# Local attention scores as 64-column products of two heads, sums by column halves, and a new order of steps

## The chip, the core and the metric

The kernel runs on one core of a Trainium2 chip. Five engines work side by side, each with its own queue of instructions: TensorE (PE; its loads of stationary weights are shown apart as PEld), VectorE (DVE), ScalarE (ACT), GpSimd (POOL) and SyncE (SP), which here issues nearly all DMA transfers. The metric is the device time of one execution in microseconds.

## The reference

Eight batches of eight heads, 576 positions, 64 features per head. Attention has two parts that are added, and then a mixture of experts works on the 4,608 tokens of 512 features:

```python
    out_d = sm_attn(q_d, k_d, v_d)          # q, k, v averaged over groups of 4: 144 positions
    out_up = np.repeat(out_d, factor, axis=2)
    mask = np.abs(pos[:, None] - pos[None, :]) < factor
    scores = scale * np.matmul(q, k.transpose(0, 1, 3, 2))
    scores = np.where(mask, scores, -1000000000.0)
    ...
    out_local = np.matmul(attn, v)          # each position sees 7 neighbours
    return (out_up + out_local)
    ...
    logits = x @ w_gate                     # 8 experts, each takes 576 tokens in order of the logits
    h = np.maximum(x[mask] @ w1[e], 0.0); out[mask] = h @ w2[e]
```

## The kernel before

The program has two stages. The first is the whole attention with the router's logits; it is what the change touches. The second routes the tokens and runs the eight experts, and begins on TensorE at 271.8 us of the profiled span.

**What the attention does per batch.** q and k arrive with positions on partitions and are turned by TensorE (`trw`, L291; the last 64 positions by `trt`, L318). ACT or DVE bring them out of PSUM (`evac`, L268 and L270; the last positions L326 and L333): k goes into `kt`, with the even head of a pair on partitions 0 to 63 and the odd one on 64 to 127; q goes into `qz`, which has a plane for each of the two heads and zeros in the other head's partitions, so that a product over 128 partitions gives one head's scores. `gsum` (L257, L260) adds groups of four positions of q and k: DVE for batch 0, POOL for the rest of q. The averaged attention, here called the means, is `down_s` (products L346, L349), `down_t` (transposes L382, L386) and `down_v` (products with the averaged v, L405, L408, L416), then a store to DRAM.

**What it does per unit.** The local part is cut into 36 units u of four windows of 32 queries by 38 keys, for all eight heads. `loc_s`: a bf16 product (L485) writes the mask for all 128 rows and 304 columns into PSUM, then 32 fp32 products (L492) add the scores, each for one head and one window: 32 columns of weights, 38 moving columns, at one of four column strips of the array. DVE takes the maximum (L502) and subtracts it (L508), ACT exponentiates (L511). `loc_t` transposes the result (L521), ACT brings it out (L529). `loc_v` multiplies with v (L544, 64 weight columns by 65), DVE normalizes (L555, L557). `log_a` adds the means, `logits` transposes the sum (L583), ACT copies it (L589), and products with 64 weight columns and 8 moving ones (L597) give the logits.

**How products count in the trace.** An fp32 product stands in the trace as two MATMUL records, each with its own weight load; a transpose or a bf16 product is one. So the 36 x 32 score products are 2,304 records. In the trace a form such as `128*32` gives the rows and columns of the array that an instruction uses; by it there are three kinds here: 128, 64 and 32 columns wide. Where two neighbours in TensorE's queue differ in that width, this text speaks of a border.

**What sets the order.** Every piece of work is a stream of steps, with a rank for each step in the table `KEYS`: `S_u`, `T_u`, `V_u` are `loc_s`, `loc_t`, `loc_v` of unit u; `X_u` the logits; `B`, `C`, `E` with a part and a batch are `down_s`, `down_t`, `down_v`; `R` and `Q` the transposes of q and k; `N` and `W` the loads. The planner always runs the step with the least rank, after whatever it needs, and each engine's queue holds the instructions in that order: in the attention this fixes the order on PE, DVE, ACT, POOL and SP alike. Engines take their queues strictly in order, so a step that is ranked too early holds up all behind it.

## Time and profile before

| | us |
|---|---|
| three runs | 731.86, 738.87, 736.12; median 736.12 |
| profiled execution | 733.37, of which 731.7 are the span that the trace shows |
| attention on TensorE | 0 to 271.8 |
| TensorE busy over the span | 662.4 (91%) |

The trace gives for each engine what it did and when; times in it count from the start of the span. Busy time of TensorE is the union of its records, which overlap, so the price of a product is better read from the distance between the starts of consecutive groups than from the duration of one record. "Idle before" names what ended the idle time of an engine; "issue" is idle time in which the engine waited for nothing that the profile shows.

### The profile page before, as it was taken

What the parts mean: (1) busy time and instruction counts of PE and PEld (TensorE: products, weight loads), DVE (VectorE), ACT (ScalarE), POOL (GpSimd) and SP (SyncE); (2) the same over time, 40 slices, a digit from 0 to 9 for tenths busy, and PEclk for the clock granted to TensorE, in tenths of its full rate; (3) what the DMA queues carried; (4) which work ended last, traced back from release to release, by engine and by line L of the source; (5) the groups of instructions that cost most, each with busy time, mean ns of one, the idle gap of its engine ahead of it and who ended that gap; (6) DMA issues with size and microseconds to landing.
All of it is one profiled execution on the core that took longest, in us unless ns stands there. A gap on an engine that the chain in (4) does not pass through costs nothing.

```text
span 731.7 us, 21463 instructions
## 1 busy us (share of the span) xinstructions
PE 662.4 (91%) x8833; PEld 473.0 (65%) x8833; DVE 492.2 (67%) x1363; ACT 346.6 (47%) x673; POOL 244.6 (33%) x296
## 2 busy tenths in 40 slices
PE   6898989899988983499999999999999999999994
PEld 4777779798867872376476576575576565674651
DVE  4876756587575756879889889698797895410300
ACT  6587757578776540433533525344253265411210
POOL 7578072835637350400612312230230441101011
PEclk9799998999999995589999999999999999999998
DMA  7899889997996560715726565182651998101001
GB/s 214 214 221 256 257 239 240 260 281 207 272 226 174 166 191 11 249 47 191 210 58 220 152 232 144 67 301 67 220 169 52 336 260 204 37 1 44 22 29 37
DMA packets 142813, 123.98 MB, mean 169 GB/s; under 512 B 86836, under 2 KB 117044, under 8 KB 142716
## 3 DMA queue, kind: packets, MB, share of 16 engines
q1 hardware_dynamic: 135256, 100.82, 48.0%
q0 software_dynamic: 6512, 21.24, 9.0%
q8 instruction: 70, 1.15, 0.7%
q10 hardware_dynamic: 948, 0.55, 0.3%
q14 instruction: 27, 0.22, 0.1%
HBM read 93.09 MB, written 21.23 MB: 156 GB/s over the span
## 4 chain that ended last, share of the span: by engine, by line
PE 52%; issue 16%; DVE 15%; POOL 5%; DMA 5%; ACT 4%; SPq 1%; POOLq 0%; DVEq 0%; ACTq 0%
PE pX L1296 13%; PE pH L1241 12%; PE o L544 4%; PE g L492 3%; PE g L291 3%; PE pR L786 2%; DVE ht L1273 2%; PE g L583 2%; POOL out_dram L1317 2%; PE g L521 2%; PE g L597 2%; PE g L346 2%; DVE cmp L753 2%; DMA nat<-in_k_dram 2%; PE g L408 2%
## 5 line engine op out<-in xcount | busy, mean ns | idle before, releaser
L1241 PE MATMUL pH<-xt,wh 128*128 128x256 f16 (+1 forms) x1024 | 194.0, 288 | 3.8 <-DVE ht L1273 2.9
L1296 PE MATMUL pX<-wh,ht 128*128 128x512 f16 (+1 forms) x640 | 183.1, 379 | 0.9 <-ACT y L1313 0.9
L1241 PE MATMUL pH<-xt,wl 128*128 128x256 f16 (+1 forms) x512 | 147.5, 288 | 0.0
L1296 PEld LDWEIGHTS <-ht 128*128 128x128 f16 (+1 forms) x960 | 80.4, 100 | 88.1 <-issue 3.7
L1296 PE MATMUL pX<-wl,ht 128*128 128x512 f16 (+1 forms) x320 | 119.0, 380 | 0.0
L1317 POOL DMA_INDIRECT out_dram<-y,idx x40 | 40.8, 1021 | 226.2 <-ACT y L1313 195.9
L1241 PEld LDWEIGHTS <-wh 128*128 128x128 f16 x1024 | 95.2, 98 | 31.2 <-DVE ht L1273 5.2
L1269 ACT ACTIVATE ht<-pH 128x512 f16<-128x512 f32 (+1 forms) x128 | 45.5, 407 | 116.1 <-PE pH L1241 103.8
L1273 DVE SCALAR_TENSOR_TENSOR ht<-pH,ht 128x512 f16<-128x512 f32 (+1 forms) x128 | 52.3, 449 | 64.4 <-ACT ht L1269 64.2
L1158 DVE SCALAR_TENSOR_TENSOR wl<-nat,wh 128x512 f16<-128x512 f32 x128 | 86.1, 684 | 1.2 <-ACT wh L1155 0.5
L1313 ACT ACTIVATE y<-pX 128x512 f32<-128x512 f32 (+1 forms) x40 | 23.7, 595 | 99.3 <-PE pX L1296 40.9
L1155 ACT ACTIVATE wh<-nat 128x1024 f16<-128x1024 f32 x64 | 67.0, 1054 | 6.2 <-DMA nat<-in_moe_w_dram 5.3
L1182 POOL DMA_INDIRECT xg<-x_dram,idx x40 | 45.6, 1140 | 62.0 <-DVE idx L1062 29.0
L1241 PEld LDWEIGHTS <-wl 128*128 128x128 f16 x512 | 50.4, 98 | 13.5 <-issue 0.4
L529 ACT COPY pt<-g 64x512 f32<-64x512 f32 x72 | 41.8, 580 | 20.4 <-PE g L521 19.4
L291 PE MATMUL g<-ident,nat 128*128 128x128 f32 x256 | 40.3, 294 | 7.5 <-DMA nat<-in_k_dram 4.9
L544 PE MATMUL o<-vw,pt 128*64 128x65 f32 x1152 | 44.3, 227 | 2.8 <-DVE gtmp L257 2.0
L544 PEld LDWEIGHTS o<-vw,pt 128*64 128x64 f32 x1152 | 38.7, 139 | 6.3 <-issue 4.0
L492 PEld LDWEIGHTS g<-kt,qz 128*32 128x32 f32 x2304 | 26.7, 113 | 20.9 <-issue 18.1
L492 PE MATMUL g<-kt,qz 128*32 128x38 f32 x2304 | 32.8, 205 | 7.9 <-issue 5.9
L291 PEld LDWEIGHTS g<-ident,nat 128*128 128x128 f32 x256 | 30.4, 149 | 11.2 <-issue 3.6
L225 POOL TENSOR_TENSOR gtv<-nat 128x512 f32<-128x512 f32 x16 | 21.4, 1338 | 46.6 <-DMA nat<-in_v_dram 24.3
(215 smaller groups left out, 1119.8 us busy)
## 6 DMA issues: line engine op xcount, KB each, us to landing
nat<-in_moe_w_dram SPq DMA_DIRECT2D x28, 1024.0 KB
vw<-in_v_dram SPq DMA_DIRECT2D x136, 78.0 KB
up<-up_dram SPq DMA_DIRECT2D x36, 256.0 KB
x_dram<-x SPq DMA_DIRECT2D x36, 256.0 KB
nat<-in_q_dram SPq DMA_DIRECT2D x16, 512.0 KB
nat<-in_k_dram SPq DMA_DIRECT2D x16, 512.0 KB
nat<-in_v_dram SPq DMA_DIRECT2D x16, 512.0 KB
up_dram<-xu SPq DMA_DIRECT2D x16, 128.0 KB
```

The lines of the kernel that those rows point to most:

```text
L291: nc.tensor.transpose(p[:, a, :, fp], src[:, 4 * hh + 2 * a + s, 2 * fp:2 * fp + 2].rearrange("p f d -> p (f d)"), self.ident)
L492: nc.tensor.matmul(sv[32 * a:32 * a + 32, 4 * g + c], self.qz[b % 2][:, h // 2, h % 2, QW * w:QW * w + QW], self.kt[b][:, h // 2, key0(w): ...
L529: nc.scalar.copy(out[r, :, :, a], p[r].rearrange("p (i h q) -> p i h q", h=4, q=QW))
L544: nc.tensor.matmul(o[64 * i:64 * i + 64, g, 65 * h:65 * h + 65], pt[:, 2 * g + i, h].rearrange("p b q -> p (b q)"), self.vw[u % 4][:, i, 4 ...
L1155: nc.scalar.activation(hi, r, AF.Copy, scale=sc)
L1158: nc.vector.scalar_tensor_tensor(lo[:, a:a + LOP], r[:, a:a + LOP], sc, hi[:, a:a + LOP], op0=OP.mult, op1=OP.subtract)
L1182: self.fetched = self.nc.gpsimd.indirect_dma_start(out=xg[:n], out_offset=None, in_=self.x, in_offset=bass.IndirectOffsetOnAxis(ap=idx[:n, ...
L1241: nc.tensor.matmul(p[:, s, :s1 - s0], self.w[k, d][a][:, 128 * f:128 * f + 128], self.xt[k][:, b, d, s0:s1], start=j == 0, stop=j == len(s ...
L1269: nc.scalar.activation(hi, q, AF.Relu)
L1273: nc.vector.scalar_tensor_tensor(lo, q, 0.0, hi, op0=OP.max, op1=OP.subtract)
L1296: nc.tensor.matmul(p[o:o + m], self.ht[k][:, f, h0:h0 + m], self.w[k, 4 + f // 2][b][:, 512 * (f % 2):512 * (f % 2) + 512], start=j < part ...
L1317: i = nc.gpsimd.indirect_dma_start(out=self.out, in_=y[:n], in_offset=None, out_offset=bass.IndirectOffsetOnAxis(ap=plan.vals["idx", k][:n ...
```

## The change

`qz` is laid out anew: per head pair and window, the 32 queries of the even head and then the 32 of the odd head lie side by side. A score product takes both as 64 columns of weights, against the same 38 keys; the zeros keep the heads apart, and the rows of the result stand where they stood. A unit has 16 score products instead of 32. The mask product of a unit, and the two kinds of products in `down_v` that were 128 columns wide (L405 and L408), are each issued as two products of 64 columns, for rows 0 to 63 and 64 to 127. The writers and readers of `qz` follow its layout: `evac` of q writes runs of 16 elements (each second one of a window of 32) instead of one run of 256; the copies of the last positions become two of 8 groups each instead of one of 16; the first addition of `gsum` reads window by window. And 505 rows of `KEYS` are written anew: all of the attention's but a dozen. The ranks of routing and experts are as before.

In the changed kernel line numbers after L250 are up to 10 higher: L291 becomes L292, L318 L324, L346 L353, L382 L389, L405 L414, L408 L418, L416 L426, L485 L496, L492 L502, L521 L531, L544 L554, L583 L593, L597 L607.

```diff
--- before.py
+++ after.py
@@ -82,7 +82,8 @@
         self.sd = cst.tile([128, 9, G], F32, name="sd")
         self.sdt = cst.tile([128, 2 * H, GT], F32, name="sdt")
         for i in range(2):
-            for name, n, l in (("qz", S, self.qz), ("qdz", 128, self.qdz), ("qdt", G - 128, self.qdt)):
+            self.qz.append(cst.tile([128, HP, NW, 2, QW], F32, name=f"qz{i}"))
+            for name, n, l in (("qdz", 128, self.qdz), ("qdt", G - 128, self.qdt)):
                 l.append(cst.tile([128, HP, 2, n], F32, name=f"{name}{i}"))
 
 
@@ -99,8 +100,8 @@
         nc = self.nc
 
         def heads(a, b, t):
-            a.memset(t[:64, :, 1], 0.0)
-            b.memset(t[64:, :, 0], 0.0)
+            for e, r, s in ((a, slice(0, 64), 1), (b, slice(64, 128), 0)):
+                e.memset(t[r, :, :, s] if len(t.shape) == 5 else t[r, :, s], 0.0)
 
         if part == 0:
             for t in self.vw[:2]:
@@ -249,12 +250,12 @@
                 self.kdt[b] = self.wk.tile([128, HP, G], F32, name="kdt")
             parts = [(slice(0, 128), self.kt[b], [(self.kdt[b], 0, G)])]
         else:
-            parts = [(slice(64 * s, 64 * s + 64), self.qz[b % 2][:, :, s],
+            parts = [(slice(64 * s, 64 * s + 64), self.qz[b % 2][:, :, :, s],
                       [(self.qdz[b % 2][:, :, s], 0, GM), (self.qdt[b % 2][:, :, s], GM, G)]) for s in range(2)]
         for i, (r, src, dst) in enumerate(parts):
             tmp = self.wk.tile([128, GW, 2 * G], F32, name="gtmp", bufs=1)[r]
             sv = src[r, a:a + GW]
-            eng.tensor_tensor(tmp, sv[..., ::2], sv[..., 1::2], op=OP.add)
+            eng.tensor_tensor(tmp.rearrange("p a (w i) -> p a w i", w=NW) if which == "q" else tmp, sv[..., ::2], sv[..., 1::2], op=OP.add)
             for d, g0, g1 in dst:
                 t = tmp[..., 2 * g0:2 * g1]
                 eng.tensor_tensor(d[r, a:a + GW], t[..., ::2], t[..., 1::2], op=OP.add)
@@ -298,10 +299,15 @@
         if which == "q":
             self.need(("fixed", b % 2))
         r = slice(64 * s, 64 * s + 64)
-        t = self.qz[b % 2][r, 2 * hh:2 * hh + 2, s] if which == "q" else self.dest(b)[r, 2 * hh:2 * hh + 2]
         for par in range(2):
-            self.evac(8 * b + 4 * hh + 2 * s + "qk".index(which) + 1, t[:, :, par:4 * GM:2],
-                      p[64 * par:64 * par + 64].rearrange("p a i f -> p a (i f)"))
+            src = p[64 * par:64 * par + 64]
+            if which == "q":
+                out = self.qz[b % 2][r, 2 * hh:2 * hh + 2, :4 * GM // QW, s, par::2]
+                src = src.rearrange("p a (w i) f -> p a w (i f)", i=QW // 4)
+            else:
+                out = self.dest(b)[r, 2 * hh:2 * hh + 2, par:4 * GM:2]
+                src = src.rearrange("p a i f -> p a (i f)")
+            self.evac(8 * b + 4 * hh + 2 * s + "qk".index(which) + 1, out, src)
             if par:
                 self.done(("tr", b, which, hh, s), g)
             yield
@@ -329,8 +335,9 @@
         self.need(("fixed", b % 2))
         for s in range(2):
             r = slice(64 * s, 64 * s + 64)
-            q = self.qz[b % 2][r, :, s, 4 * GM:].rearrange("p h (g f) -> p f g h", f=4)
-            self.nc.scalar.copy(q, p[r, :, 0])
+            for w in range(2):
+                q = self.qz[b % 2][r, :, 4 * GM // QW + w, s].rearrange("p h (g f) -> p f g h", f=4)
+                self.nc.scalar.copy(q, p[r, :, 0, 8 * w:8 * w + 8])
             if s:
                 self.done(("ttq", b), g)
             yield
@@ -402,11 +409,14 @@
         pt = self.ptd[b]
         o, gi = self.galloc()
 
-        nc.tensor.matmul(o[:, :260], pt[:, 9], vd[:, 1, 4 * g:4 * g + 4].rearrange("p h d -> p (h d)"),
-                         start=True, stop=False, skip_group_check=True)
+        HALVES = (slice(0, 64), slice(64, 128))
+        for r in HALVES:
+            nc.tensor.matmul(o[r, :260], pt[:, 9, r], vd[:, 1, 4 * g:4 * g + 4].rearrange("p h d -> p (h d)"),
+                             start=True, stop=False, skip_group_check=True)
         for j in range(4):
-            nc.tensor.matmul(o[:, 65 * j:65 * j + 65], pt[:, 4 * g + j], vd[:, 0, 4 * g + j],
-                             start=False, stop=True, skip_group_check=True)
+            for r in HALVES:
+                nc.tensor.matmul(o[r, 65 * j:65 * j + 65], pt[:, 4 * g + j, r], vd[:, 0, 4 * g + j],
+                                 start=False, stop=True, skip_group_check=True)
         if g:
 
             for i in range(2):
@@ -482,16 +492,16 @@
             if g == 0:
                 self.need("mask")
                 s, gi = self.galloc()
-                nc.tensor.matmul(s[:, :H * KW], self.identb, self.mask[:, None, ukind(u)].to_broadcast([128, 2, 4 * KW]),
-                                 start=True, stop=False, skip_group_check=True)
+                for r in (slice(0, 64), slice(64, 128)):
+                    nc.tensor.matmul(s[r, :H * KW], self.identb[:, r], self.mask[:, None, ukind(u)].to_broadcast([128, 2, 4 * KW]),
+                                     start=True, stop=False, skip_group_check=True)
                 sv = s[:, :H * KW].rearrange("p (g c k) -> p (g c) k", g=2, k=KW)
             for c in range(4):
                 b, w = divmod(4 * u + c, NW)
-                for a in range(4):
-                    h = 4 * g + a
-                    nc.tensor.matmul(sv[32 * a:32 * a + 32, 4 * g + c], self.qz[b % 2][:, h // 2, h % 2, QW * w:QW * w + QW],
-                                     self.kt[b][:, h // 2, key0(w):key0(w) + KW], start=False, stop=True,
-                                     skip_group_check=True, tile_position=(0, 32 * a))
+                for a in range(2):
+                    nc.tensor.matmul(sv[64 * a:64 * a + 64, 4 * g + c], self.qz[b % 2][:, 2 * g + a, w].rearrange("p s q -> p (s q)"),
+                                     self.kt[b][:, 2 * g + a, key0(w):key0(w) + KW], start=False, stop=True,
+                                     skip_group_check=True)
             if g:
                 self.done(("sp", u))
             yield
...
-    "B00": [144, 155, 157, 161, 162],
-    "S_12": [658, 662, 674, 680, 694, 695],
-    "T_11": [698, 711, 716, 717],
-    "T_12": [761, 766, 779, 780],
...
+    "B00": [86, 95, 100, 106, 107],
+    "S_12": [657, 662, 669, 673, 684, 685],
+    "T_11": [706, 721, 725, 726],
+    "T_12": [690, 705, 708, 709],
...
```

Three places on TensorE show how the instructions stand. The first is the start, from the second unit's scores to the third unit's transposes of batch 0 (`sw_119` holds the exponentials of even units, `sw_120` those of odd ones). Before:

```order
L492 MATMUL g<-kt,qz_107 32x38 x32
L485 LDWEIGHTS identb
L485 MATMUL g<-mask,identb 128x304
L492 MATMUL g<-kt,qz_107 32x38 x32
L521 MATMUL g<-ident,sw_119 128x128 x4
L318 MATMUL g<-ident,natt 64x128 x8
L521 MATMUL g<-ident,sw_120 128x128 x4
```

Now:

```order
L502 MATMUL g<-kt,qz_107 64x38 x16
L353 MATMUL g<-kdt,qdz_108 128x144 x3
L496 LDWEIGHTS identb
L496 MATMUL g<-mask,identb 64x304
L496 LDWEIGHTS identb
L496 MATMUL g<-mask,identb 64x304
L502 MATMUL g<-kt,qz_107 64x38 x16
L531 MATMUL g<-ident,sw_119 128x128 x4
L531 MATMUL g<-ident,sw_120 128x128 x4
```

The first products of the means (L353, once L346) have moved ahead of the third unit's scores, and nothing stands between the transposes of units 0 and 1.

The second place is in the middle: before, the scores of unit 14 and what follows to the transposes of unit 13.

```order
L485 LDWEIGHTS identb
L485 MATMUL g<-mask,identb 128x304
L492 MATMUL g<-kt,qz_111 32x38 x32
L544 MATMUL o<-vw_118,pt_122 64x65 x16
L597 MATMUL g<-wgf,xt 64x8 x8
L291 MATMUL g<-ident,nat 128x128 x4
L583 MATMUL g<-ident,x 128x128 x4
L382 MATMUL g<-ident,sd 128x128 x3
L521 MATMUL g<-ident,sw_120 128x128 x4
```

Now, the scores of unit 12 and what follows to the transposes of units 12 and 11:

```order
L496 LDWEIGHTS identb
L496 MATMUL g<-mask,identb 64x304
L496 LDWEIGHTS identb
L496 MATMUL g<-mask,identb 64x304
L502 MATMUL g<-kt,qz_107 64x38 x16
L554 MATMUL o<-vw_116,pt_122 64x65 x16
L292 MATMUL g<-ident,nat 128x128 x4
L607 MATMUL g<-wgf,xt 64x8 x8
L531 MATMUL g<-ident,sw_119 128x128 x4
L554 MATMUL o<-vw_117,pt_121 64x65 x16
L593 MATMUL g<-ident,x 128x128 x8
L531 MATMUL g<-ident,sw_120 128x128 x4
```

Before, a unit's transposes stood behind the next unit's scores; here unit 12's stand behind its own, and ahead of those of unit 11.

The third place is a batch's products with the averaged v, near the end of the attention. Before:

```order
L597 MATMUL g<-wgf,xt 64x8 x8
L405 MATMUL g<-vd_114,ptd 128x260
L408 MATMUL g<-vd_114,ptd 128x65 x4
L405 MATMUL g<-vd_114,ptd 128x260
L408 MATMUL g<-vd_114,ptd 128x65 x4
L416 MATMUL g<-vd_114,ptd 32x65 x16
L521 MATMUL g<-ident,sw_119 128x128 x4
```

Now:

```order
L607 MATMUL g<-wgf,xt 64x8 x8
L414 MATMUL g<-vd_114,ptd 64x260 x2
L418 MATMUL g<-vd_114,ptd 64x65 x8
L414 MATMUL g<-vd_114,ptd 64x260 x2
L418 MATMUL g<-vd_114,ptd 64x65 x8
L426 MATMUL g<-vd_114,ptd 32x65 x16
L607 MATMUL g<-wgf,xt 64x8 x8
```

The width changes at other places now: behind the products of 8 columns (64 wide) there is no border any more. Over the whole attention, borders in TensorE's queue number 189 before and 191 now.

## Rows read from the trace of the kernel before

**Rows 1.** Windows: PE, PEld, DVE, ACT, POOL busy (instructions), PEclk, DMA share, GB/s.
```profile
20.00:60.00 40.00, 35.50 (x744) 29.76 (x734) 30.22 (x59) 29.00 (x58) 25.30 (x34) 0.89 0.91 224
60.00:140.00 80.00, 70.96 (x1602) 62.72 (x1598) 51.50 (x116) 54.48 (x108) 41.62 (x53) 0.96 0.90 247
140.00:230.00 90.00, 84.57 (x1984) 74.53 (x1984) 63.88 (x138) 67.14 (x133) 48.61 (x62) 0.98 0.91 247
230.00:272.00 42.00, 38.56 (x995) 34.50 (x996) 25.47 (x75) 20.81 (x44) 18.83 (x32) 0.99 0.54 163
```

**Rows 2.** TensorE's waits to 272 us: us in total, times, longest.
```profile
PE g L492 <- issue: 5.9, 7, 1.9
PE g L291 <- DMA nat<-in_k_dram: 4.9, 3, 2.5
...
PE g L521 <- DVE rx L555: 0.7, 1, 0.7
...
PE g L408 <- issue: 0.6, 1, 0.6
```

**Rows 3.** Groups of TensorE's products: busy us, mean ns, idle before.
```profile
L544 PE MATMUL o<-vw,pt 128*64 128x65 f32 x1152 | 44.3, 227 | 2.8 <-DVE gtmp L257 2.0 <-DVE x L557 0.4 <-PE g L492 0.2
L492 PE MATMUL g<-kt,qz 128*32 128x38 f32 x2304 | 32.8, 205 | 7.9 <-issue 5.9 <-ACT kt L270 2.0
L597 PE MATMUL g<-wgf,xt 128*64 128x8 f32 x576 | 22.3, 203 | 0.2 <-ACT xt L589 0.2
```

**Rows 4.** Timeline of TensorE: start us, us, instruction, form, count.
```profile
41.62 0.48 PE L492 MATMUL g<-kt,qz 128*32 128x38 f32 x32
42.03 0.66 PE L521 MATMUL g<-ident,sw 128*128 128x128 f32 x4
...
146.33 0.69 PE L544 MATMUL o<-vw,pt 128*64 128x65 f32 x16
146.85 0.59 PE L597 MATMUL g<-wgf,xt 128*64 128x8 f32 x16
147.37 0.66 PE L291 MATMUL g<-ident,nat 128*128 128x128 f32 x4
...
151.26 0.29 PE L485 MATMUL g<-mask,identb 128*128 128x304 bf16 x1
151.48 0.79 PE L492 MATMUL g<-kt,qz 128*32 128x38 f32 x64
152.20 1.15 PE L544 MATMUL o<-vw,pt 128*64 128x65 f32 x32
153.18 0.59 PE L597 MATMUL g<-wgf,xt 128*64 128x8 f32 x16
...
157.92 1.00 PE L408 MATMUL g<-vd,ptd 128*128 128x65 f32 x8
158.85 1.15 PE L544 MATMUL o<-vw,pt 128*64 128x65 f32 x32
159.83 1.04 PE L318 MATMUL g<-ident,natt 128*64 128x128 f32 x16
160.71 0.59 PE L597 MATMUL g<-wgf,xt 128*64 128x8 f32 x16
```

**Rows 5.** Groups of the other engines up to 272 us.
```profile
L529 ACT COPY pt<-g 64x512 f32<-64x512 f32 x72 | 41.8, 580 | 20.4 <-PE g L521 19.4
L270 ACT COPY qz<-g 64x512 f32<-64x512 f32 x52 | 32.9, 632 | 6.4 <-PE g L291 5.8
...
L508 DVE TENSOR_TENSOR sw<-g,mx 128x304 f32<-128x304 f32 x36 | 17.1, 475 | 2.4
L502 DVE TENSOR_REDUCE mx<-g 128x8 f32<-128x304 f32 x36 | 16.9, 470 | 14.1 <-PE g L492 13.8
L511 ACT ACTIVATE sw<-sw 128x304 f32<-128x304 f32 x36 | 16.5, 458 | 24.5 <-DVE sw L508 24.3
...
L333 ACT COPY qz<-g 64x256 f32<-64x256 f32 x16 | 10.3, 642 | 0.2
```

1002 rows, old and new, of the table KEYS are left out of this document.

## The prediction

> **What bounds the kernel now.** I read the windows first, to see where in the program the changed engines are short of time. From 20 to 272 us TensorE is busy for 229.6 of 252 us and idle for 4.5, 9.0, 5.4 and 3.4, together 22.4 [rows 1]. DVE and ACT are at about 70% there (64 and 67 of 90 us between 140 and 230), POOL at half. The DMA engines are 0.90 busy up to 230 us, so loads are a second limit close behind, and from 230 us on TensorE alone is full. So in this stage a microsecond of TensorE's work, added or removed, is nearly a microsecond of time. Routing and experts keep their order and move as a block. Then the waits, to see what the idle time is: the largest entry is 5.9 us before score products that waited for nothing the profile shows ("issue"), next 4.9 us for loads of k [rows 2]. Then the groups, and the timeline for prices from start to start, since records overlap.
>
> **Scores: plus 11.2.** Thirty-two records of the 32-column form take 0.41 us until the next group starts, and sixty-four take 0.72; each time a border is in it, so 32 more cost 0.31, and a unit of 64 costs 0.62 [rows 4]. What 64 columns with 38 moving ones cost isn't in the trace; two rows enclose it. With 65 moving columns, sixteen records take 0.52 and thirty-two 0.98, a border each: 0.46 for 16, or 29 ns a record. With 8 moving columns sixteen take 0.52 as well, the same [rows 4]. Since 8 and 65 moving columns cost alike, 38 will too: the pace is set by the 64 columns of weights. A unit's 32 records then cost 0.93, so 0.31 more, and 36 units 11.2 us. The groups' busy times say nearly the same: 14.2 ns a record for the old form, 38.5 and 38.7 for the two 64-column forms [rows 3], so 1.23 against 0.91 a unit, 11.7 in all. Halving the count of products does not pay here, because two strips of 64 load no faster than four strips of 32 that load side by side.
>
> [...]
>
> **Sums by halves: minus 6.1.** [...] The 260-column product and the mask I cost at nothing: 16 records of 64 columns by 128 moving ones take 0.88 us [rows 4], 110 ns a pair, so two halves run side by side at the pace of one whole product and streaming sets the time.
>
> **Borders: plus 0.2, at most plus 1.7.** [...] More of them lead to or from the 64 wide form, whose first pair also comes about 0.05 late (0.98 for thirty-two records against 0.93 by pitch); some thirty more such entries bound this at 1.7.
>
> **Instruction stalls: minus 5.** The 5.9 us of "issue" before score products are seven stops, up to 1.9 us, and L408 has 0.6 [rows 2]; the two 64-column groups list none in 1,728 records [rows 3]. The old score run takes a MATMUL record and a load each 9.7 ns, the new one each 29 ns, so the queue is drained at a third of the pace. If the pace makes the stops, 6.5 goes; if they sit at fixed places in the program, nothing. I take 5, since the lines that already run at the new pace have none.
>
> **Writers and readers of qz: nothing.** ACT's 52 copies of q write runs of 16 instead of 256. Runs of 32 cost nothing (580 ns for 512 elements against 632 for the q copy now), runs of 4 double the price (642 ns for 256) [rows 5]; the new copy lies between 0.58 and 1.28 us, and I take 0.63, near the runs of 32. The 16 copies of the last positions become 32 of half the size, between 0.32 and 0.64 us each: 0 to 10 us of ACT's time in 272. POOL's first additions read the same elements in shorter runs. ACT and POOL have about 30% and 45% free time in the stage [rows 1]; should that cover go, the third rival below is what it costs.
>
> **The order: nothing, within minus 8 and plus 9.** Apart from the instruction stops, 16.5 us of TensorE's idle time are left. A new order can take out half of them or add as much again; no row prices it, so it widens the range and doesn't move the middle.
>
> **Sum.** 11.2 - 6.1 + 0.2 - 5 = +0.3; half the extra of late first pairs makes it +1. The profiled execution took 733.4 (span 731.7), so 734.4 on that scale; the median of the three runs is 2.7 above it, and on its scale the forecast is 737. About 1% (7.4 us) is what a measurement of this kernel can tell from no change.
>
> **Rivals.**
>
> *Slower: transposes that stand too close behind their scores.* A unit's transposes need maximum, subtraction and exponential first: 0.47 + 0.48 + 0.46 = 1.4 us of work on DVE and ACT [rows 5], with three hand-overs and whatever stands ahead in their queues. Now unit 12's transposes follow its own scores after one group of v products, four transposes and eight logit products, about 2 us by [rows 4], where before the next unit's scores came between. Laying such prices along both orders, 13 units have less than 4 us between scores and transposes, against 2 before. Where the slack is under the chain's real length, TensorE stands with everything queued behind the transpose, as in the one wait of 0.7 us that such transposes show now [rows 2]. Thirteen units at 0.7 are 9 us: 746. For it: DVE and ACT are 70% busy, so their queues are seldom empty. Against it: the same order also fixes DVE's and ACT's queues, and may serve these chains first. It decides if the mean wait of these units is over 0.5 us. Chance 0.22.
>
> *Slower: the stops stay.* If instruction stops belong to places, not to pace, the sum is +6 and the time 742, still within 1%; with the upper bound of the borders 743.5. Chance 0.12, half of it beyond 1%.
>
> *Slower: ACT.* With q copies at 1.28 us, ACT gets 34 us more on the 171 of 252 us that it is busy [rows 1], 81%, and its copies of k and q, on which the transposes' buffers wait, come late. It decides above some 0.9 us a copy. I give it 6 us, 743; chance 0.06.
>
> *Faster: the order fills idle time.* In the new start the first products of the means stand before the third unit's scores and fill time in which TensorE waited for k (4.9 us in three waits [rows 2]). If half of the remaining 16.5 us goes so, the time is 729, and with all stops gone 727. Against it: nothing loads earlier, since the first dozen transfers on SP stand as before. Chance 0.18.
>
> *Faster: fewer drains.* [...] Chance 0.02.
>
> **Numbers.** The forecast, 731 to 743 with 737 as its middle, has a chance of 0.4. Low end 727 is the faster rival with all stops gone, high end 750 the close transposes at 1 us each on top of the sum. Faster than 728.7: 0.18. Slower than 743.5: 0.22 and halves of the two smaller ones, less what of them falls inside, 0.27. The same: 0.55.
>
> **What would show it.** The score line as 1,152 records, 0.93 us from its start to the next group; the v-sum line at half its 0.93; no or little "issue" before scores; L291 to L597 at their present pitch; routing starting at 273 us (271.8 now). Waits of the transposes (L531) for DVE or ACT of more than 3 us in all would show the first rival, a q copy above 0.9 us the third. The forecast is wrong if the new score records run clearly under 29 ns, since then 64 columns of weights aren't what sets the pace, or if the stage's idle time apart from stops leaves 9 to 26 us.

## The result and the profile after

The changed kernel took 727.18 us (median of 4 runs, 722.1 to 729.47) against 734.40 for the kernel before: ratio 0.988, 95% interval 0.9836 to 0.9924. Later comparisons of the same program gave 0.9929 (0.9896 to 0.9961, 12 runs), and a copy with other warm-up products 0.9951 (0.9921 to 0.9981). So the change is worth 4 to 9 us, where 1 us more was forecast. The size is near what one comparison can tell, the direction is not in doubt. 727.18 lies just inside the range, at the low end that one rival gave it, which is luck: the middle of the forecast lay on the other side of no change.

The profiled execution took 722.1 us (span 720.5). Routing started at 262.8 us instead of 271.8; routing and experts took 457.7 us after that, against 459.9. So the gain is in the attention. The windows of the kernel after, columns as in [rows 1]:

```profile
20.00:60.00 40.00, 35.33 (x580) 29.74 (x580) 28.84 (x57) 30.49 (x67) 27.31 (x37) 1.00 0.87 220
60.00:140.00 80.00, 76.74 (x1487) 67.14 (x1486) 59.32 (x131) 58.41 (x120) 43.77 (x54) 1.00 0.90 243
140.00:230.00 90.00, 84.91 (x1642) 74.93 (x1639) 59.33 (x135) 66.40 (x135) 45.26 (x57) 0.98 0.92 249
230.00:262.00 32.00, 30.47 (x670) 26.44 (x665) 19.54 (x61) 16.67 (x34) 19.35 (x27) 1.00 0.71 214
```

In this profile TensorE isn't busier in the first stretch, but its granted clock is 1.00 there and in the next, where it was 0.89 and 0.96. Two later profiles in the same order have 0.92 and 0.94 in the first and 1.00 in the next. In the last stretch the DMA engines are 0.71 busy instead of 0.54: more of the transfers now fall there. TensorE's waits to 262 us (total, times, longest):

```profile
PE g L292 <- DMA nat<-in_k_dram: 6.5, 7, 1.8
PE g L292 <- DMA nat<-in_q_dram: 4.1, 4, 1.5
...
PE g L502 <- issue: 0.6, 1, 0.6
...
PE g L531 <- ACT sw L521: 0.4, 1, 0.4
```

Of before, [rows 2] show the wait for k; this is the one for q:

```profile
PE g L291 <- DMA nat<-in_q_dram: 2.3, 1, 2.3
```

In this profile loads of k and q are waited for longer than before (10.6 against 7.2 us), in eleven short waits instead of four; in the two later profiles it is 4.9 and 3.9 us, in five waits and three. The seven stops before scores, 5.9 us, are down to one of 0.6. The transposes behind their scores wait 0.4 us in all. Groups of the kernel after, to 262 us (busy us, mean ns, idle before):

```profile
L554 PE MATMUL o<-vw,pt 128*64 128x65 f32 x1152 | 43.4, 224 | 0.4
L502 PE MATMUL g<-kt,qz 128*64 128x38 f32 x1152 | 41.5, 226 | 2.0 <-ACT kt L271 1.4 <-issue 0.6
...
L271 ACT COPY qz<-g 64x512 f32<-64x512 f32 x52 | 32.0, 615 | 8.6 <-PE g L292 7.9
...
L340 ACT COPY qz<-g 64x128 f32<-64x128 f32 x32 | 10.5, 433 | 0.2
```

Busy time of the score line went up by 8.7 us, half the products [rows 3]. The q copies cost 615 ns instead of 632, the 32 half-size ones together 10.5 us instead of 10.3 [rows 5]. And TensorE's timeline after, where the new forms' prices can be read from start to start:

```profile
152.03 0.66 PE L414 MATMUL g<-vd,ptd 128*64 128x260 f32 x4
152.52 0.64 PE L418 MATMUL g<-vd,ptd 128*64 128x65 f32 x16
152.99 0.61 PE L414 MATMUL g<-vd,ptd 128*64 128x260 f32 x4
...
159.07 0.30 PE L496 MATMUL g<-mask,identb 128*64 128x304 bf16 x2
159.21 1.08 PE L502 MATMUL g<-kt,qz 128*64 128x38 f32 x32
160.11 0.62 PE L607 MATMUL g<-wgf,xt 128*64 128x8 f32 x16
```

Sixteen halves of sums take 0.47 us (eight whole ones took 0.93), a unit's scores 0.90 (0.72 [rows 4]), and from mask to scores 0.14 pass instead of 0.22.

**A balance of the attention.** For every kernel below I split the time up to the first routing product into four. *Stops*: TensorE's idle time ended by "issue". *Waits*: its other idle time (pauses over 60 ns). *Low clock*: where the granted clock is 0.5, the start-to-start time above the median of the same pair of lines at full clock. *Products*: the rest. In us, a mean where there are several profiles (one of the three of after is that of the copy with other warm-up products):

```
kernel (profiles)               routing at  products  low clock  stops  waits   ratio of times to before
before (2)                        273.4       232.2      11.0      8.4   21.9   1.0013
sums by halves alone (2)          274.6       226.4      12.3     12.3   23.6   1.0161, 1.0029
scores alone (1)                  270.6       235.8      12.1      3.0   19.7   1.0011
both forms, old order (2)         268.5       230.4      12.2      4.5   21.5   0.9996, 0.9992
order alone (1)                   272.5       239.2       5.0      7.1   21.1   0.9999
order and scores, whole sums (1)  264.4       243.4       3.8      0.0   17.2   0.9943
after (3)                         261.5       238.1       4.5      1.2   17.6   0.988, 0.9929, 0.9951
```

One profile differs from the next of the same program by up to 4 us here; the runs' ratios have intervals of about 0.4% to either side. The profiles of the order alone and, below, of the narrow scores are of slow runs, 1.5% and 3.3% above the shortest of their kernel, and the ratios leave such runs out.

In the old order the stops hold one wait that is no stop for instructions (see "Are the loads the cause?"): 3.6 us in one of the two profiles of before, 1.7 in one of the sums alone, 3.0 in the scores alone, 4.0 in each of both forms. The rest of the stops of before comes to 6.6 us in the mean.

### The profile page after: what moved, and what is told of

The parts are those of the page before. It is cut to its first block, busy times and chain, and to the rows that moved or that the text cites. A ratio compares the mean times of both kernels' runs of the same rounds, so it can differ in the third digit from the quotient of the medians.

```text
span 720.5 us, 19570 instructions
## 1 busy us (share of the span) xinstructions
PE 658.3 (91%) x7877; PEld 469.1 (65%) x7877; DVE 490.9 (68%) x1363; ACT 347.0 (48%) x689; POOL 247.0 (34%) x296
## 3 DMA queue, kind: packets, MB, share of 16 engines
q8 instruction: 62, 1.02, 0.6%
## 4 chain that ended last, share of the span: by engine, by line
PE 44%; DVE 17%; issue 16%; DMA 12%; ACT 4%; POOL 3%; SPq 3%; POOLq 0%; ACTq 0%; DVEq 0%
PE pX L1306 13%; PE pH L1251 11%; DMA nat<-in_k_dram 5%; PE o L554 3%; PE g L502 2%; PE pR L796 2%; DVE ht L1283 2%; POOL out_dram L1327 2%; PE g L292 2%; ACT kt L271 2%; DMA up<-up_dram 2%; DVE cmp L763 2%; DMA nat<-in_q_dram 1%; PE g L593 1%; PE g L607 1%
## 5 line engine op out<-in xcount | busy, mean ns | idle before, releaser
L1251 PE MATMUL pH<-xt,wh 128*128 128x256 f16 (+1 forms) x1024 | 192.0, 286 | 4.7 <-DVE ht L1283 2.8
L258 POOL TENSOR_TENSOR gtmp<-qz 64x576 f32<-64x576 f32 x28 | 33.5, 1198 | 62.9 <-ACT qz L340 41.0
L292 PE MATMUL g<-ident,nat 128*128 128x128 f32 x256 | 37.5, 284 | 12.0 <-DMA nat<-in_k_dram 6.5
L554 PE MATMUL o<-vw,pt 128*64 128x65 f32 x1152 | 43.4, 224 | 0.4
L502 PE MATMUL g<-kt,qz 128*64 128x38 f32 x1152 | 41.5, 226 | 2.0 <-ACT kt L271 1.4
L502 PEld LDWEIGHTS g<-kt,qz 128*64 128x64 f32 x1152 | 40.3, 138 | 3.7 <-issue 2.1
L554 PEld LDWEIGHTS o<-vw,pt 128*64 128x64 f32 x1152 | 37.9, 137 | 4.8 <-issue 3.7
L292 PEld LDWEIGHTS g<-ident,nat 128*128 128x128 f32 x256 | 28.4, 144 | 16.8 <-issue 7.1
```

Of the source, the lines that this page charges most:

```text
L292: nc.tensor.transpose(p[:, a, :, fp], src[:, 4 * hh + 2 * a + s, 2 * fp:2 * fp + 2].rearrange("p f d -> p (f d)"), self.ident)
L502: nc.tensor.matmul(sv[64 * a:64 * a + 64, 4 * g + c], self.qz[b % 2][:, 2 * g + a, w].rearrange("p s q -> p (s q)"), self.kt[b][:, 2 * g + ...
L554: nc.tensor.matmul(o[64 * i:64 * i + 64, g, 65 * h:65 * h + 65], pt[:, 2 * g + i, h].rearrange("p b q -> p (b q)"), self.vw[u % 4][:, i, 4 ...
L1251: nc.tensor.matmul(p[:, s, :s1 - s0], self.w[k, d][a][:, 128 * f:128 * f + 128], self.xt[k][:, b, d, s0:s1], start=j == 0, stop=j == len(s ...
```

## Experiments

**Again, unedited.** The kernel before, and the changed one.

> The kernel before once more, unedited, for the spread of one profile to the next and of the comparison itself. If its falls of the clock and its stops belong to the program, this profile shows 20 to 32 us at the lower clock before routing, 5 to 12 us of stops and routing at 269 to 275 us again; its expert stage, which was short in the first profile (423.4 us against 425 to 429 in most others), comes out at 425 to 428. If they are chance, either sum differs by more than a half. Ratio 0.996 to 1.004.

> The changed kernel once more, nothing edited. If its short low-clock time (3.4 us) and short instruction stops (1.1 us) belong to the program, the profile shows both again within 3 us and the ratio is 0.985 to 0.992. If they are a matter of the single run (which transfers happen to be under way), this profile shows other places and more of both, and the ratio lies nearer to 1 (0.990 to 1.000).

Before: 735.43 us, ratio 1.0013 (0.9976 to 1.0051), routing at 274.9, 25.9 us at the lower clock, stops 9.8. After: 728.93 us, 0.9929, routing at 262.4, 11.0 us at the lower clock, stops 2.4. In the kernel before, falls and stops belong to the program in their sum (24.2 and 6.9 us in the first profile). The after's first profile was lucky in the start (3.7 us at the lower clock in all): the second lost 6.8 us of clock at 19.3.

**The two halves of the change.** The changed kernel with the whole table of before (one line of it stands here), and the kernel before with the new table:

```
-    "B00": [86, 95, 100, 106, 107],
+    "B00": [144, 155, 157, 161, 162],
...
```

> The changed kernel's products and layout of qz, run in the order of steps of the kernel before. Theory A (the order made the gain, by cutting the long waits behind which TensorE's clock fell to its lower level): the forms alone are worth 0 us within 3: about 6 us more of TensorE's work, 5 to 6 us fewer instruction stops, and the clock still falls in the start and near 108 us, with over 10 us at the lower level before 260 us. Theory B (the forms made it, since fewer instructions keep TensorE fed): 6 to 9 us faster than before, no stops, little time at the lower level.

> The kernel before (32-column scores, whole sums and mask) in the new order of steps. Theory A: 4 to 8 us faster than before, less than 10 us at the lower clock level in the attention, instruction stops of about 5 us still there. Theory B: no faster than before, within 2 us, or slower.

Forms: 730.86 us, 0.9996 (0.9958 to 1.0033). Order: 734.91 us, 0.9999 (0.9957 to 1.004). Theory A had given the order alone 4 to 8 us, theory B the forms alone 6 to 9. Neither half gives anything by itself: the gain needs both. Forms once more:

> Both forms in the old order, once more and unedited. Its first profile had routing at 266.7 us, 5.1 sooner than the kernel before, but 3.6 us more in the expert stage (one wait for the transposed rows of 3.4 us), and the ratio was 0.9996. If the expert stage's wait is a matter of the single run, it differs here (0 to 4 us), routing starts at 264 to 269 us, and over both jobs the ratio comes to 0.994 to 0.999. If the old order brings that wait itself, it is 3 to 4 us again and the ratio 0.998 to 1.003.

732.66 us, 0.9992 (0.9954 to 1.003), routing at 270.3, and the expert stage's wait is 4.2 us again. In the balance both profiles have routing 1.5 to 8 us sooner than those of before, of which the runs show hardly anything. The expert stage took 426.7 to 430.6 us in all four profiles of both forms or of the scores alone in the old order at full loads, 423.4 and 424.7 in those of before, 421.7 to 429.1 in those of after; it differs by one wait for the transposed rows xt. Why that wait varies stays open.

**One form at a time.** The edit takes the halves away again, in both forms and in the changed kernel; its reverse in the kernel before gives the sums alone. The 260-column product is edited likewise:

```
-            for r in HALVES:
-                nc.tensor.matmul(o[r, 65 * j:65 * j + 65], pt[:, 4 * g + j, r], vd[:, 0, 4 * g + j],
+            nc.tensor.matmul(o[:, 65 * j:65 * j + 65], pt[:, 4 * g + j], vd[:, 0, 4 * g + j],
```

> The kernel before with one edit: the products with the averaged v (L405, L408) as column halves, old order. By the price of the prediction 6 us of TensorE's work go; if TensorE bounds the attention, 4 to 6 us faster; if loads or other waits take the place of that work, 0 to 2 us faster. The L408 group falls from 0.84 to 0.46 us either way.

> The kernel before with the scores (and the mask) by 64-column products alone, the sums whole and the order as before. Theory W, the prediction's sum: scores +11, stops -5, so some 6 us later, routing at 276 to 279 us, ratio 1.006 to 1.010. Theory S: the score products at a wider pitch take away the stops and with them falls of the clock, which are worth more than the prediction's 5 us: routing at 268 to 273 us, stops under 4 us, ratio 0.995 to 1.002.

> The changed kernel with one part undone: the sums of the means are whole products of 128 columns again, as before; order, scores and mask stay as changed. Theory W (product time decides, as in the prediction's sum): TensorE's product time before routing rises by 5.5 to 6.1 us, routing starts at 266 to 269 us instead of 259 to 263, the ratio to the kernel before is 0.998 to 1.003. Theory S (the products by halves pay with stops and falls of the clock what they save, as they did alone in the old order, where product time fell 5.6 us and the time rose): routing starts at 258 to 263 us, ratio 0.988 to 0.995.

Sums alone: 740.8 us, 1.0161 (1.0099 to 1.0224), slower although products fell by 5.8 us. Scores alone: 734.13, 1.0011 (0.9969 to 1.0052). After without the halves: 730.35, 0.9943 (0.9905 to 0.9981), level with after. So the sums' halves save product time as forecast and next to no time of the kernel; the scores cost product time and no time.

**Narrow scores in the changed kernel.**

```
-                for a in range(2):
-                    nc.tensor.matmul(sv[64 * a:64 * a + 64, 4 * g + c], ...
+                for a in range(4):
+                    nc.tensor.matmul(sv[32 * a:32 * a + 32, 4 * g + c], ... tile_position=(0, 32 * a))
```

> The changed kernel (new order, new layout of qz, sums by halves) with the scores again as 32 products of 32 columns and the mask as one product. If the wide scores cost what the prediction said (0.31 us a unit) and their only return is fewer instruction stops and fewer borders (about 9 us), this is about as fast as the changed kernel, within 3 us, with some 4 to 6 us of stops back. If the wide scores are what made the change fast, it is 4 us or more slower than the changed kernel (727).

734.01 us, 0.9982 (0.9928 to 1.0037): without the wide scores the new order gains nothing. Of its 16.6 us of stops only the direction is used.

**Stops: place or pace.** The 13 warm-up products of 512 columns became 52 of 128, in the changed kernel and in "sums only"; and the changed kernel got as many score records as the kernel before:

```
-NWARM = 13
+NWARM = 52
...
-                nc.tensor.matmul(p, w, w[:, None].to_broadcast([128, 4, 128]), start=True, stop=True)
+                nc.tensor.matmul(p[:, :128], w, w, start=True, stop=True)
```
```
                 for a in range(2):
+                    for n in (0, KW // 2):
...
```

> The changed kernel with its 13 warm-up products of 512 columns cut into 52 of 128 columns: the same columns, but 78 instructions more ahead of everything on TensorE, so that every boundary of 256 instructions, where the stops for instructions stand, falls at another place of the program. Theory P, the place of a boundary decides whether its packet comes late: the stops before routing go from 1.1 us to 4 to 12 us, some of over 2 us with a fall of the clock behind them, and the ratio to the kernel before rises from 0.988 to 0.993 to 1.003. Theory Q, order and number of instructions (the pace) decide, as the prediction had it: stops stay under 3 us and the ratio within 0.985 to 0.992.

> The kernel before with the sums of the means by halves alone (which had taken 5.6 us of product time off TensorE and came out 1.6% slower, with 12.8 us of stops and 32 us at the lower clock), now with the same 78 instructions of warm-up more ahead of everything. Theory P (places): the stops come at other boundaries and fall to 4 to 9 us, and the ratio goes from 1.016 to 0.995 to 1.008. Theory Q (the form itself makes the stops): stops of 11 us or more and a ratio of 1.012 to 1.020 again.

> The changed kernel with each 64-column score product split into two over 19 keys each: as many instructions as the kernel before has in its scores (2,304 products), but at the wider pitch of the 64-column weights (some 27 to 29 ns each). TensorE's work rises by at most 36 x 0.93 = 33 us for this. Theory pace (a stop comes when instructions go by faster than their packets are fetched): stops before routing stay under 4 us. Theory number (more instructions, more packets, more stops): stops come back to 7 us or more. Time under either: ratio 1.02 to 1.045, by the added score time less what other waits give back.

After, shifted: 730.17 us, 0.9951; stops 0.1 us. Sums only, shifted: 736.2 us, 1.0029 (1.0 to 1.0057); stops 11.7 us where there were 12.8, at other lines. So the boundaries move the places, not the sum. Split scores: 759.32 us, 1.0353 (1.0288 to 1.0418). Its waits of TensorE by "issue" before routing are two:

```profile
PE o L555 <- issue: 0.3, 1, 0.3
PE g L503 <- issue: 0.3, 1, 0.3
```

Those of the sums alone, shifted, of 1 us or more in all:

```profile
PE o L547 <- issue: 6.2, 5, 3.1
...
PE g L419 <- issue: 2.4, 2, 2.1
...
PE g L586 <- issue: 1.2, 1, 1.2
...
PE g L411 <- issue: 1.0, 1, 1.0
```

With 2,304 score records at the wide pitch the stops come to 0.6 us; with 2,304 at the narrow one they come to 6 to 12, and to 7.1 in the new order with the old forms. It is the pace, as the prediction assumed. The split also added 31.5 us to TensorE's product time (238.1 to 269.6) and, by the ratios, 32 us to the time. That the sums alone lost 1.6% in one copy and 0.3% in the other, with the same stops, isn't explained.

**Is the clock the cause?** Idle products of ones, of 512 columns each, were put into TensorE's longest waits (products of 512 columns start 216 ns apart at a clock of 1.00 in the trace of before, L1296):

```
+    def fill(self, o, n):
+        for _ in range(n):
+            self.nc.tensor.matmul(o, self.wm, self.wm[:, None].to_broadcast([128, 4, 128]), start=True, stop=True)
...
         p, g = self.galloc()
+        self.fill(p, FR.get((which, hh, s, b), 0))
```

> The kernel before, its order and its forms, with 30 bf16 products of ones (128x512, some 0.22 us each at full clock, no result of theirs is used) put into TensorE's queue where its four longest waits stood: 8 ahead of the first k transposes (wait of 2.53 us at 12.5), 7 between the halves of the first block's scores (1.98 us at 18.7), 8 ahead of the first q transposes of batch 4 (2.32 us at 108.1), 7 ahead of the value products of block 14 (1.98 us at 140.1). Nothing is taken out. Theory A, the clock: the falls after these waits (24 us at the lower level, some 10 to 11 us of extra time) are what the changed order avoids. Then the time at the lower level before routing falls under 10 us, the first routing product comes at 264 to 267 us instead of 271.8, and the time is 5 to 8 us shorter (ratio 0.989 to 0.993). Theory B, the clock doesn't decide, since the loads and the other engines set the pace of those stretches: other idle time grows by what the clock gives back, routing starts at 270 to 274 us, ratio 0.998 to 1.005.

> Both forms in the old order (two profiles: 27 and 34 us at the lower clock, 10 to 14 us of extra time, routing at 266.7 and 270.3 us), with 32 idle bf16 products of ones put where its long waits stand: 8 ahead of the first k transposes, 4 between the halves of the first block's scores, 8 ahead of the first q transposes of batch 4, 12 ahead of the value products of block 15. [...] Theory A (falls of the clock are worth their extra time): the lower clock falls to under 12 us and routing starts at 259 to 264 us, ratio 0.988 to 0.995. Theory B (the loads set the pace, and the time that a higher clock gives back is waited for elsewhere): the lower clock falls too, but idle time grows, routing starts at 266 to 271 us, ratio 0.998 to 1.005.

> The changed kernel with 11 such idle products in its two longest waits of the start (6 ahead of the first k transposes, 5 between the halves of the first block's scores), where two of its three profiles show a fall of the clock (6.8 us at the lower level). Theory A: that fall goes, routing starts at 256 to 260 us, ratio to the kernel before 0.983 to 0.990. Theory B: the next load swallows it, as the start of the filled kernel before showed (2 us ahead after the first three blocks, nothing left at the fourth): routing at 259 to 263 us, ratio 0.989 to 0.996.

Before, filled: 740.04 us, 1.0057 (1.0019 to 1.0095), 28.8 us at the lower clock, at other places. Forms, filled: 733.54, 1.0011 (0.9986 to 1.0037). After, filled: 728.32, 0.9936 (0.9909 to 0.9964), a time as without; its profile has 13.1 us at the lower clock and routing at 265.8, later than either theory said. So the filling cut the time at the lower clock in the forms alone, and only they test the theories. The windows of the forms in the old order, unfilled, show the start that the filling was to mend:

```profile
0.00:20.00 20.00, 13.90 (x115) 9.76 (x116) 8.65 (x24) 11.46 (x20) 14.96 (x25) 0.85 0.82 229
20.00:60.00 40.00, 38.62 (x620) 33.34 (x619) 30.88 (x62) 31.14 (x67) 27.33 (x37) 0.90 0.94 242
60.00:140.00 80.00, 71.19 (x1354) 64.12 (x1354) 54.56 (x120) 54.38 (x113) 43.42 (x55) 0.94 0.94 255
```

And the same windows, filled:

```profile
0.00:20.00 20.00, 16.69 (x169) 10.43 (x171) 9.37 (x26) 12.03 (x21) 15.38 (x26) 1.00 0.85 233
20.00:60.00 40.00, 33.91 (x556) 29.12 (x553) 30.81 (x60) 29.18 (x64) 24.88 (x34) 0.96 0.90 237
60.00:140.00 80.00, 73.79 (x1367) 65.08 (x1366) 55.16 (x120) 54.53 (x112) 44.88 (x57) 0.95 0.95 257
```

The clock rose from 0.85 to 1.00 and from 0.90 to 0.96, and TensorE then stood still for longer (33.91 busy against 38.62): the fourth block was normalised at 56.8 us, against 55.4 and 58.3 in the two unfilled profiles. From 20 to 60 us TensorE waited 4.8 us for loads of k, against 0.9 and 3.5 us unfilled, with the DMA engines 0.90 to 0.94 busy: there the loads took the place of what the clock gave. Extra time at the lower clock fell from 12.2 to 6.9 us, routing started at 267.9 instead of 268.5. The theory that each fall of the clock costs the kernel its extra time foretold 259 to 264 us and a ratio of at most 0.995, and missed both. It isn't refuted for good: the idle products raised the product time by 7 us, and no run shows how much of what the clock gave back went into them.

**Are the loads the cause?** Three of the four windows of v that a block loads were left out, in three kernels; the value products then read what the tile held:

```
-            for r0, n in ((0, VR),) if k0 + VR <= S else ((0, 32), (32, KW - 32)):
+            for r0, n in () if c else ((0, VR),) if k0 + VR <= S else ((0, 32), (32, KW - 32)):
```

> The kernel before without three of the four windows of v that each local block loads (L491's products then read what was in the tile; 102 of the 136 transfers, which are most of the packets under 512 B, are left out); every instruction of the engines stays. Theory L (the loads set the waits, with them the falls of the clock, and their packets stand ahead of those with instructions): waits of TensorE before routing fall from 22 to under 13 us, the time at the lower clock from 24 to 26 us to under 12, the stops from 7 to 10 us to under 4; routing starts at 250 to 258 us. Theory O (the order of the engines' own hand-overs makes the waits): waits stay above 17 us, routing at 262 to 272 us.

> Both forms in the old order, with the same three of four windows of v left out. Product time in the old order is 230 us against 238 in the new one. Theory L: with the loads light the old order loses its handicap, waits fall from 21 to under 12 us, low clock under 10, routing starts at 244 to 252 us and the time is equal to or up to 8 us shorter than that of the changed kernel made light in the same way. Theory O: it stays 4 to 8 us longer than that one.

> The changed kernel with the same three of four windows of v left out. Theory L: product time stays at 238 us, waits fall from 17.6 to under 12 us, routing starts at 249 to 254 us, later than or level with the light kernel of the old order. Theory O: routing at 244 to 250 us, 4 to 8 us ahead of it.

Packets took 178 us of each DMA engine's time before routing instead of 229. Light, the kernel before took 728.55 us, ratio 0.992 (0.9886 to 0.9954), the forms in the old order 722.73, 0.9845 (0.9794 to 0.9897), the changed one 723.23, 0.9844 (0.9804 to 0.9883). So with the loads light, the order makes no difference to the time (0.6% at full loads), and the forms alone give 0.75% (nothing at full loads). The window from 60 to 140 us of the light forms in the old order:

```profile
60.00:140.00 80.00, 73.30 (x1416) 66.61 (x1416) 58.62 (x126) 57.61 (x118) 42.81 (x54) 0.96 0.74 230
```

And of the light kernel after:

```profile
60.00:140.00 80.00, 78.12 (x1515) 68.35 (x1514) 58.08 (x131) 59.03 (x124) 44.14 (x54) 1.00 0.75 234
```

With the DMA engines at 0.75 the old order still has the lower clock and less busy time. In the times this is as the loads' theory has it; the sizes in the profiles are not. Waits fell to 17.0, 16.1 and 14.2 us only, routing started at 260.1, 257.9 and 254.5, and the new order is still 3.5 us ahead there. In these profiles it loses that lead behind the attention (464.2 against 460.9 us), where the wait for xt is 4.5 us against 1.3. So the equal times don't show that light loads take away all that the order gives.

In seven profiles of the old order, with full loads and with light ones, TensorE waits 1.7 to 4.1 us before block 15's value products. The wait stands as "issue", but it is no instruction stop: it isn't a multiple of 256 instructions from the stops, and it ends up to 7.5 us after the last instruction packet landed. In the light forms, first DVE, then TensorE:

```profile
127.81 0.76 DVE L258 TENSOR_TENSOR gtmp<-kt 128x576 f32<-128x576 f32 x1 [3.96 <-POOL qdt L261]
...
131.57 0.69 DVE L567 TENSOR_TENSOR x<-o,rx 128x512 f32<-128x512 f32 x1
```
```profile
132.36 1.14 PE L554 MATMUL o<-vw,pt 128*64 128x65 f32 x16 [4.05 <-issue]
```

By the program a block's value products may begin only when DVE has normalised the block before (L567), since `o` has one buffer. In all seven profiles that normalisation ended 0.07 us before TensorE loaded its next weights. DVE was late because an addition of k stands ahead of it in its queue, and this addition waited 2.3 to 4.0 us for POOL: both use `gtmp`, which has one buffer too. In the rows above the addition starts at 127.81 us and the normalisation behind it at 131.57. Over the whole attention DVE's additions of k, before and after:

```profile
L257 DVE TENSOR_TENSOR gtmp<-kt 128x576 f32<-128x576 f32 x9 | 7.8, 869 | 13.2 <-POOL qdt L260 13.1
```
```profile
L258 DVE TENSOR_TENSOR gtmp<-kt 128x576 f32<-128x576 f32 x9 | 7.8, 866 | 2.5 <-ACT kt L271 1.9 <-POOL kdt L261 0.5
```

No profile of the new order has a wait of DVE for `qdt`, and none has the wait at block 15. At 4.05 us it is as large as the lead of 3.5 us that is left with light loads. No run changes this hand-over alone, so its price in time isn't shown.

## Why the prediction was wrong

By lines of TensorE's product time (start to start, full clock; means of the profiles in the balance):

```
line                        before   forms, old order   after    the prediction's term
scores                       27.7          34.3          35.6     +11.2
mask                          8.1           5.4           5.3       0
sums of 65 columns           19.3          13.4          13.4      -6.1
sums of 260 columns           8.2           7.4           7.4       0
all others, warm-up too     168.9         169.9         176.4     borders +0.2, order 0
```

**The order: nothing.** This step failed. The prediction said that no row priced the order, and left it at nothing. It costs 7.0, 7.6 and 7.7 us of product time (with old forms, with the scores, with both): its table has 44 to 50 more borders in TensorE's queue for the same forms (189 to 239, 147 to 191), at 0.08 us each some 4 us by estimate, and v products alone take 39.5 us instead of 36.3. It gives back 6 to 8 us of low clock in every pair, and, once the scores are wide, 2.5 to 4 us of waits and 3 of stops, which are the wait at block 15: 6 to 7 us in the attention, some 5 us of the time. Three terms that can outweigh the borders were in view. DVE's 13.1 us of waiting for POOL weren't read, though they stand in the view from which [rows 5] are taken. A clock of 0.89 and 0.96 [rows 1] was never made a term, although each of the four falls in the attention of before (at 12.1, 19.0, 107.7 and 141.8 us, to 0.5) came in an idle time of TensorE of 1.98 to 2.53 us or up to 1.7 us behind one. The DMA engines, 0.90 busy to 230 us and 0.54 after, were named "a second limit" without asking what an order that moves transfers into the last stretch would give. How far the falls of the clock are the loss and how far they only go along with waits for loads isn't settled; filling waits moved one without the other.

**"A microsecond of TensorE's work is nearly a microsecond of time."** This premise failed for work taken away: sums by halves took 5.8 us away in the old order and the time rose, and the forms save 0.75% with light loads and nothing with full ones. For work added it held, in the one case that was run: the split scores added 31.5 us of it to the changed kernel and 32 us of time.

**Scores: plus 11.2.** Right was that a record of 64 weight columns costs about as much with 38 moving columns as with 8 and with 65 (0.52 us for sixteen of either [rows 4]); the size was not. The pitch is 27.6 ns a record, not 29 (mean over records whose next is a score too), and the line rose by 6.6 us in the old order. Of the 4.6 us between, 1.6 are the pitch. Most of the rest is the border behind the scores: a whole unit took 0.72 us up to the v products with it, and takes 0.90 without. The mask by halves, put at nothing, gave 2.7 back: mask and scores share one width, and from the one to the other pass 0.14 us instead of 0.22; the 0.08 between I take for a border's price. No run halves the mask alone. So fewer borders did pay, the rival called "fewer drains", whose chance was 0.02 (no trace shows a drain, only the 0.08 us). The count of borders, 189 and 191, told against it, but it was a sum of two: the forms take 42 away, the order adds 44. Net cost 4, not 11.2. Loads of weights overlap in both forms: in the trace of before 64 loads of 32 columns, 0.11 us each, took 0.67 us together, 32 of 64 columns, 0.14 us each, 1.02 us (PEld at 151.48 and 152.20).

**Sums: minus 6.1.** I took a border's price off the whole products for this term, which no run shows by itself. In its place the runs show 5.9 of work, and 0.8 more for the 260 columns; of the time little came.

**Borders: plus 0.2.** No run shows this term either: it was my estimate for two borders more. The runs show the 0.08 us between mask and scores. An estimate from the trace of before comes near that: at 216 ns for 512 columns (L1296) the mask's 304 take 0.13 of the 0.22 us up to the scores, which leaves 0.09.

**Stops: minus 5.** Right, size and reason: without the wait at block 15, 6.6 to 1.2 us, and pace it is. That lines at the wide pitch have none was luck of the first trace: in the second profile of before two stops, 1.4 and 0.8 us, stand in the value products.

**Writers and readers of qz: nothing.** Right: 615 ns, and 10.5 us for the small copies.

**The rivals.** Close transposes: no, 0.4 us of waits, 1.4 in another profile. Stops stay: no. ACT: no. The order fills idle time: the one that came, but mostly not in the start, where its reason was. From 60 to 140 us idle time fell from 9.0 and 5.2 us to 3.3, 2.5 and 1.9, and the balance's 6.5 us of low clock were no part of it. Its 0.18 was too little; a table with other ranks at almost every step deserved bounds from rows that show a second limit.

## What to carry to other kernels

Read the clock and the DMA share of every window as terms: in the kernel before, with a clock of 0.89 to 0.98 and the DMA engines 0.90 to 0.91 busy from 20 to 230 us, 5.8 us of work taken off TensorE by the sums' halves did not come back as time (ratios 1.0161 and 1.0029), though 31.5 us added to the changed kernel cost 32. Count borders apart for each part of a change, since two parts can cancel in the count, as the 42 and 44 did here. Read also how long the other engines wait for each other: here DVE waited 13.1 us for POOL over one shared buffer, and TensorE's queue stood behind it, up to 4.1 us, with nothing named. In the trace of before the clock stood at 0.5 for 24.2 us, with idle times of TensorE at each fall, yet raising the clock with idle products (0.85 to 1.00 and 0.90 to 0.96) gave no time in the one kernel where it rose (ratio 1.0011).

## What the runs showed of the hardware

- The pages list instruction packets on a queue (q8): 1.15 MB in 70 packets before, 1.02 MB in 62 after, 16.4 KB each. TensorE has 17,666 and 15,754 records of products and loads there, 252 and 254 to a packet without those for semaphores, so I take the queue for TensorE's. Most stops by "issue" stand 256 instructions apart or a multiple of it (in the trace of before those at 23.66, 65.00, 78.22 and 129.05 us are 1,536, 512 and 2,048 apart), and end 1.3 to 1.7 us after a packet landed, which had started with at most 211 instructions left to issue (182 in the two profiles of before). With the DMA engines 0.9 busy they come to 6 to 12 us where score records start every 10 ns, and to 0 to 2.4 us at 28 ns; with them at 0.75, in the light kernel before, to 3.7 us at 10 ns.
- ACT's copy of 64 x 128 took 433 ns where one of 64 x 256 took 642.
